# A fused attention and two-MLP kernel: SBUF tiles moved to 512-byte starts, A's four slices set 1280 bytes apart

## The chip, the cores and the metric

The kernel runs on one core of one Trainium2 chip. Each of the core's partitions of SBUF (there are 128) holds its share of every tile as a run of bytes; where in the partition a tile starts is decided when the program is built. The metric is device time in microseconds (us) of one execution, the median of several runs.

## What is computed

All tensors are fp32. A Nystrom attention (4 batches, 8 heads, 576 tokens, head size 64, 32 landmarks) is followed by two MLPs on 2304 tokens of width 512:

```
q_lm, k_lm = means over 32 segments of 18 tokens
A, Bm, C   = softmax(q k_lm'), softmax(q_lm k_lm'), softmax(q_lm k')
Z          = six Newton steps towards the inverse of Bm
x          = A @ Z @ C @ v
x          = rms_norm(x) * g ;  y = (silu(x @ w_gate) * (x @ w_val)) @ w_out      # d_ff 1536
h          = y @ w_in ;         out = (s * relu(h)**2 + b) @ w_out2               # d_ff 2048
```

## The kernel before

One function builds the whole program. Every step is recorded as an operation with the engines it may run on, an estimated duration and a key; a list scheduler (class `Scheduler`, `run`) then issues the operations in an order that is fixed at build time. Each engine walks its own list and waits on semaphores.

The large products use three fp32r matmuls for one fp32 product. `split` (lines 1115 to 1121) cuts an operand into a high part (L1117 on ScalarE or L1118 on VectorE) and a low part (L1119), and the matmuls add high times high, high times low and low times high (`PART3`, line 1244). Each of them loads its own 128x128 block of weights, the stationary operand, and then streams 256, 288 or 512 columns, the moving operand, past it. The matmul lines in question are:

- L1326 in `first_mm` (line 1319), the first MLP's gate and value products. Moving: a slice of A, 288 columns, from a tile of `xh` (high) or `xl` (low). Stationary: u (weights with the attention folded in), from `u_all` or from the free columns of `xh` and `xl`. 4 batches x 12 blocks of d_ff x 2 halves x 2 parts x 6 = 1152 matmuls.
- L1390 in `out_mm`, the first MLP's output product. Moving: `hh` or `hl` (the hidden block). Stationary: `w_all`. 528 matmuls of 512 columns and 144 of 256.
- L1282 in `product`, the second MLP's input product, which takes seven products instead of eight per pair of token blocks. Moving and stationary from `region`, `u_all`, `xh` and `xl`. 2 x 8 x 7 x 6 = 672 matmuls of 512 columns.
- L1417 in `second_mm`, the second MLP's output product. Moving: the output weights, from `w_all`, `region` or `u_all`. Stationary: `hh` or `hl`. 16 x 18 x 3 = 864 matmuls of 512 columns.
- L1664 in `plain`, the last token block's input product, 192 matmuls of 256 columns; moving from `region`, stationary from `xh` or `xl`.

Together that is 3552 fp32r matmuls: 2064 of 512 columns, 1152 of 288 and 336 of 256. The other matmuls (the attention's, the folding of the weights at L1299, the first blocks of the output product at L1372) are plain fp32.

A is stored in `attention` (lines 1092 to 1103). Its four slices, one for each pair of head group `g` and half `hf` of a segment, lie side by side in one tile of `xh` and one of `xl`, 288 columns (`HC`, 1152 bytes) each:

```
cols = slice(2 * HC * g + HC * hf, 2 * HC * g + HC * hf + HC)
```

SBUF is laid out in the order in which tiles are asked for, in the pool `sb` first and `region` in the pool `rp` behind it. Each tile starts at the next multiple of 32 bytes. The small tiles at the head of `sb` (masks, scalars) leave everything behind them 352 bytes past a multiple of 512, and `hmore` (3456 bytes) and `hbuf` shift what follows once more.

Of the kernel before, what the change touches and what calls it, by code (L numbers as in the profile page):

```python
# [7 lines left out]
F32 = mybir.dt.float32  # L8
F32R = mybir.dt.float32r
# [97 lines left out]
class Scheduler:  # L107
# [10 lines left out]
    def op(self, alts, key, fn, r=(), w=(), pair=False):  # L118
        if isinstance(alts, tuple):
            alts = {alts[0]: alts[1]}  # L120
        names = list(r) + list(w)
        bufs = {id(b): b for b in (x[0] if isinstance(x, tuple) else x for x in names) if isinstance(b, Buf)}
        o = Op(alts, key, fn, list(bufs.values()), pair)
        for b in o.bufs:
            b.left += 1
        deps = {}
        for x in r:
            if x in self.writer:
                deps[id(self.writer[x])] = self.writer[x]
        for x in w:  # L130
            if x in self.writer:
                deps[id(self.writer[x])] = self.writer[x]
            for y in self.readers.get(x, ()):
                deps[id(y)] = y
        for x in w:
            self.writer[x], self.readers[x] = o, []
        for x in r:
            self.readers.setdefault(x, []).append(o)
        deps.pop(id(o), None)
        for d in deps.values():  # L140
            d.users.append(o)
            o.n_deps += 1
        self.ops.append(o)
        return o
# [122 lines left out]
def t_dve(n):  # L267
    return 0.065 + 0.00104 * n


def t_dve2(n):
    return 0.07 + 0.00052 * n
# [6 lines left out]
def t_act(n):  # L279
    return 0.055 + 0.00085 * n  # L280
# [15 lines left out]
def tile_nystrom_attention_two_mlps(  # L296
# [16 lines left out]
    B, H, S, D = q.shape  # L313
    NT, DM = out.shape
    M = 32
    SEG = S // M
    HB = SEG // 2
    HC = HB * M
    NP = HC // 3
    KD = DM // 128  # L320
    F1 = w_gate.shape[1] // 128
# [10 lines left out]
    sb = ctx.enter_context(tc.tile_pool(name="sb", bufs=1))  # L332
# [3 lines left out]
    def ring(n, shape, name, dtype=F32):  # L336
        return Ring([Slot(sb.tile(shape, dtype, name=f"{name}{i}")) for i in range(n)], True)
# [11 lines left out]
    gT = sb.tile([128, KD], F32, name="gT")  # L349
    s_sb = sb.tile([128, 1], F32, name="s_sb")  # L350
    b_sb = sb.tile([128, 1], F32, name="b_sb")
    xbuf = sb.tile([128, KD, NT], F32, name="xbuf")

    x_r = [ring(2, [128, KD, 512], nm, F32R) for nm in ("xh", "xl")]
# [11 lines left out]
    u1_r = [Ring(u.slots + m, True) for u, m in zip(u_r, u_more)]  # L366
    u3_r = [Ring(u.slots + m[1:], True) for u, m in zip(u_r, u_more)]
    gw_r = ring(2, [128, 128], "gw")
    hmore = sb.tile([128, 864], F32, name="hmore")
    N_H = 8  # L370
    hbuf = sb.tile([128, 1536 + N_H * 288], F32, name="hbuf")
    t1_r = Ring([Slot(hbuf[:, 288 * i:288 * i + 288]) for i in range(2)], True)
    hs_r = [ring(2, [128, 512], nm, F32R) for nm in ("hh", "hl")]

    R_COLS, T_COLS = 11776, 3392
    rp = ctx.enter_context(tc.tile_pool(name="rp", bufs=1))
    region = rp.tile([128, R_COLS], F32, name="region", tag="region")
    tail = sb.tile([128, T_COLS], F32, name="tail")
    r_at = [0]

    def rring(n, cols, queued=True):
        o = []
        for _ in range(n):
            x, c = (region, r_at[0]) if r_at[0] < R_COLS else (tail, r_at[0] - R_COLS)
            assert c + cols <= x.shape[1], (r_at, cols)
            o.append(Slot(x[:, c:c + cols]))
            r_at[0] += cols
        return Ring(o, queued)
# [6 lines left out]
    bd_r = rring(4, 128)  # L395
    A_r = rring(2, HC)
    AT_r = rring(4, HC)
    wbd_r = rring(1, 256)
# [8 lines left out]
    tT0_r = Ring(tT_r.slots + [Slot(far[:, c, 0:SEG * D]) for c in range(2)], True)  # L407
    A0_r = Ring(A_r.slots + [Slot(far[:, 2, HC * i:HC * i + HC]) for i in range(2)] + [Slot(far[:, 3, 640:640 + HC])], True)
    h_late = [Slot(xbuf[:, c, NT - HC:NT]) for c in range(KD)]
    for x in h_late:  # L410
        x.held = True
    h_main = [Slot(hbuf[:, c:c + HC]) for c in [HC * i for i in range(2, 5)] + [1536 + HC * i for i in range(N_H)]]
    h_more = [Slot(hmore[:, HC * i:HC * i + HC]) for i in range(3)]
    hq_r = Ring(h_main + h_more + h_late, True)
    eC0_r = Ring(eC_r.slots + [Slot(far[:, 2, 576:1152])], True)
# [17 lines left out]
    for n, c in enumerate(COMBOS):  # L433
        for kd in range(2):
            i = 2 * (2 * n + kd)
# [70 lines left out]
    def attention(b, t0, t1):  # L506
# [8 lines left out]
        def at(alts, pos, fn, r=(), w=(), pair=False):  # L515
            mine.append(op(alts, 0.0, fn, r, w, pair or set(alts) == {"dve", "pool"}))
            mine[-1].spare = {"dve": SPA if b else SPA0}
            if not first and "sp" not in mine[-1].alts:
                mine[-1].after = RELB
            at_ops.append(mine[-1])  # L520
# [4 lines left out]
        def near(n):  # L525
            return {"dve": t_dve(n)} if first else dp(n)

        pair = xs[1, b] = (Buf(x_r[0]), Buf(x_r[1]))

        def part(i):  # L530
            return pair[i].t.rearrange("p k n -> p (k n)")[:, 0:SEG * D]

        def piece(g, h):

# [181 lines left out]
        for it in range(6):  # L716
            pU = Buf(ps_r)
            n = 32 if it in (2, 5) else 64
# [292 lines left out]
        for hf in range(2):  # L1011
# [22 lines left out]
            for c in range(0 if b >= XB else KD):  # L1034
                g, pr = divmod(c, 2)
# [23 lines left out]
            def s_mm(_, pS=pS, xq=xq, n_sum=n_sum):  # L1059
# [5 lines left out]
                for j in range(3):  # L1065
                    for c in range(n_sum):
                        nc.tensor.matmul(
                            out=pS.t[0:NP, j:j + 1], lhsT=xq.t[:, HC * c + NP * j:HC * c + NP * j + NP],
                            rhs=ones[:, 0:1], start=(c == 0), stop=(c == n_sum - 1))
# [4 lines left out]
            def s_rec(e, pS=pS, rs=rs):  # L1074
                e.tensor_scalar(out=rs.t[0:NP, 0:3], in0=pS.t[0:NP, 0:3], scalar1=1.0 / DM, scalar2=1e-6, op0=ALU.mult, op1=ALU.add)
                e.reciprocal(out=rs.t[0:NP, 0:3], in_=rs.t[0:NP, 0:3])

            at(("dve", 0.34), p0 + 0.06, s_rec, r=[pS], w=[rs])
            at(("act", 0.2 if first else 1.4), p0 + 0.07, lambda e, rs=rs: e.activation(
                out=rs.t[0:NP, 0:3], in_=rs.t[0:NP, 0:3], func=ACTF.Sqrt), r=[rs, "table"], w=[rs, ("root", b, hf)])  # L1080
            if first and hf:
                at(("act", 1.4), 0.0, lambda e: e.activation(out=spare, in_=spare, func=ACTF.Tanh),
                   r=[("root", 0, 0), ("root", 0, 1)], w=["spare"])
            at(near(HC), p0 + 0.07, lambda e, rs=rs, dg=dg: e.tensor_tensor(
                out=dg.t[0:NP].rearrange("p (j c) -> p j c", j=3),
                in0=ident[0:NP, 0:NP].unsqueeze(1).to_broadcast([NP, 3, NP]),
                in1=rs.t[0:NP, 0:3].rearrange("p (j o) -> p j o", o=1).to_broadcast([NP, 3, NP]),
# [3 lines left out]
                r=[dg, "const"], w=[pR])  # L1091
            for g in range(2):
                a = AT[hf, g]
                cols = slice(2 * HC * g + HC * hf, 2 * HC * g + HC * hf + HC)
                at(("dve", t_dve(HC)), p0 + 0.08, lambda e, a=a, pR=pR: e.tensor_tensor(
                    out=a.t[:, 0:HC], in0=a.t[:, 0:HC], in1=pR.t[:, 0:HC], op=ALU.mult), r=[a, pR], w=[a])
                wh, wl = ([(pair[i], ("a", hf, g))] for i in range(2))
                at({"act": t_act(HC), "dve": t_dve2(HC)}, p0 + 0.09, lambda e, a=a, cols=cols: (
                    e.activation(out=part(0)[:, cols], in_=a.t[:, 0:HC], func=ACTF.Copy) if e is nc.scalar
                    else e.tensor_copy(out=part(0)[:, cols], in_=a.t[:, 0:HC])), r=[a], w=wh, pair=True)  # L1100
                at(near(HC), p0 + 0.1, lambda e, a=a, cols=cols: e.tensor_tensor(
                    out=part(1)[:, cols], in0=a.t[:, 0:HC], in1=part(0)[:, cols].bitcast(F32),
                    op=ALU.subtract), r=[a, wh[0]], w=wl, pair=True)
                if first and g and hf:
                    at(("pool", 0.1), p0 + 0.11, lambda e, cols=cols: e.tensor_copy(
                        out=mark, in_=part(1)[:, cols][:, 0:1].bitcast(F32)), r=wl, w=["sums"])
# [212 lines left out]
    def first_mm(key, b, part, hf, u, ps):  # L1319
        x = xs[1, b]  # L1320

        def mm(_):
            for g in range(2):
                for i, (a, y) in enumerate(PART3):
                    c = 2 * HC * g + HC * hf
                    nc.tensor.matmul(  # L1326
                        out=ps.t[:, 0:HC], lhsT=u[a].t[:, 256 * g + 128 * part:256 * g + 128 * part + 128],
                        rhs=x[y].t.rearrange("p k n -> p (k n)")[:, c:c + HC],
                        start=(g == 0 and i == 0), stop=(g == 1 and i == 2))

        op(("pe", 6 * t_mm(HC)), key, mm, r=[(y, g) for y in u for g in range(2)]
           + [(y, ("a", hf, g)) for y in x for g in range(2)], w=[ps]).mode = "r"
        u_ops.append(S_.ops[-1])
# [124 lines left out]
    o_at, n = {}, 0  # L1458
    for i, (j, f) in enumerate(outs):
        lag = min(LAG0, max(LAG1, LAG0 - (i - F1) // 2))  # L1460
        n = max(n + (i >= len(units)), i + lag if i < len(units) else 0)
# [238 lines left out]
    for i, x in enumerate(todo):  # L1700
        if x[0] == "in":
            p, g = x[1:]
# [3 lines left out]
            n = 2 * (g > 0) if p == 0 else 4  # L1706
            steps = 7
        else:
            if x[1] == 0:
                x_last(t - X_LEAD)  # L1710
            g = x[1]
            n, steps = 2 if g < F_G - 1 else 2, 2
# [4 lines left out]
        keys, k = [], 0  # L1717
# [65 lines left out]
```

## Time and profile before

| | |
|---|---|
| median of 3 runs | 827.8 us (826.54 to 829.6) |
| the profiled execution | 828.2 us, of which the span of instructions is 826.5 us |
| TensorE (PE) busy | 812.0 us, 98% |
| weight loads (PEld) busy | 654.0 us, 79% |
| VectorE (DVE) busy | 644.1 us, 78% |
| ScalarE (ACT) busy | 463.2 us, 56% |
| GpSimd (POOL) busy | 122.4 us, 15% |
[...]

PE and PEld are the two halves of TensorE's work, matmuls and the loads of their weights. A matmul's duration runs from its start to the end of its results, so successive matmuls overlap and the busy time counts their union. The pace of a run of matmuls is therefore read from the distance between starts, not from one's duration.

### The profile page before, as it was taken

To read this page: it belongs to the slowest core of one execution; us is meant where nothing else is said; L and a number is where in the kernel's file an instruction comes from. 1 tells how busy PE (TensorE), PEld (TensorE's weight loads), DVE (VectorE), ACT (ScalarE), POOL (GpSimd) and SP (SyncE) were. 2 spreads that over 40 slices of the span, in tenths; PEclk is the share of its full clock that TensorE was granted. 3 is DMA by queue.
4 is the path that set the end of the run, shared out by engine and by line. 5 is a ranking of instruction groups with operands and counts; after the bars stand their busy time and mean duration, and the time that the engine had idled before them with its cause. 6 is when DMAs were issued, how large, how long until landed. Compare 5 with 4: busy or idle time off the path is not lost.

```text
span 826.5 us, 16515 instructions
## 1 busy us (share of the span) xinstructions
PE 812.0 (98%) x6158; PEld 654.0 (79%) x6158; DVE 644.1 (78%) x1452; ACT 463.2 (56%) x971; POOL 122.4 (15%) x176
## 2 busy tenths in 40 slices
PE   8999999999999999999999999999999999999997
PEld 5577777887787777888888888887888888888886
DVE  6888988777787777898998899698766767665564
ACT  5755665443535334565547766578555556565553
POOL 1370365127311132210100000000000000000000
PEclk9999999999999999999999999999999999999999
DMA  9999998352443323489888772232422432254234
GB/s 280 339 309 393 256 301 250 133 148 78 135 141 106 113 77 91 140 277 264 283 249 267 228 251 97 87 102 76 129 77 76 116 89 90 73 159 138 64 90 128
DMA packets 88817, 138.44 MB, mean 168 GB/s; under 512 B 28064, under 2 KB 50592, under 8 KB 88736
## 3 DMA queue, kind: packets, MB, share of 16 engines
q1 hardware_dynamic: 88544, 137.12, 54.4%
q8 instruction: 48, 0.79, 0.4%
q14 instruction: 33, 0.27, 0.1%
q10 hardware_dynamic: 192, 0.26, 0.1%
HBM read 114.81 MB, written 22.54 MB: 166 GB/s over the span
## 4 chain that ended last, share of the span: by engine, by line
PE 79%; DVE 8%; DMA 6%; ACT 2%; issue 1%; POOL 1%; SPq 0%; DVEq 0%; ACTq 0%; POOLq 0%
PE bank L1417 23%; PE bank L1282 16%; PE bank L1326 14%; PE bank L1390 13%; PE bank L1664 3%; PE bank L1299 2%; DMA stage<-in_moe_w_out_dram 2%; DMA xbuf<-in_moe_w_val_dram 2%; PE bank L1372 1%; DVE w_all L1119 1%; PE bank L760 1%; PE bank L681 1%; DVE hl L1119 1%; DMA rawo<-kepto 1%; POOL region L586 1%
## 5 line engine op out<-in xcount | busy, mean ns | idle before, releaser
L1417 PE MATMUL bank<-w_all,hh 128*128 128x512 f32 x472 | 148.0, 394 | 0.0
L1390 PE MATMUL bank<-hh,w_all 128*128 128x512 f32 (+1 forms) x448 | 144.7, 379 | 0.2 <-DVE w_all L1119 0.2
L1417 PEld LDWEIGHTS bank<-w_all,hh 128*128 128x128 f32 x472 | 88.2, 188 | 20.3
L1390 PEld LDWEIGHTS bank<-hh,w_all 128*128 128x128 f32 x448 | 81.5, 188 | 24.8 <-issue 10.4
L1417 PE MATMUL bank<-w_all,hl 128*128 128x512 f32 x236 | 93.1, 394 | 0.0
L1326 PE MATMUL bank<-xh,u_all 128*128 128x288 f32 x400 | 87.6, 299 | 0.3
L1390 PE MATMUL bank<-hl,w_all 128*128 128x512 f32 (+1 forms) x224 | 83.0, 371 | 0.0
L1119 DVE TENSOR_TENSOR w_all<-rawo,w_all 128x512 fp32r<-128x512 f32 x85 | 60.2, 708 | 15.9 <-ACT w_all L1117 13.4
L1326 PEld LDWEIGHTS bank<-xh,u_all 128*128 128x128 f32 x400 | 66.1, 188 | 3.8 <-issue 1.0
L1343 ACT ACTIVATE hbuf<-bank 128x288 f32<-128x288 f32 x96 | 39.2, 408 | 49.9 <-PE bank L1326 46.6
L1326 PE MATMUL bank<-xl,u_all 128*128 128x288 f32 x200 | 59.0, 295 | 0.0
L1326 PE MATMUL bank<-xh,xl 128*128 128x288 f32 x184 | 54.3, 295 | 0.0
L1326 PE MATMUL bank<-xl,xh 128*128 128x288 f32 x184 | 54.2, 295 | 0.0
L1417 PEld LDWEIGHTS bank<-w_all,hl 128*128 128x128 f32 x236 | 44.3, 188 | 10.5
L1117 ACT ACTIVATE w_all<-rawo 128x512 fp32r<-128x512 f32 x54 | 34.0, 629 | 31.3 <-PE bank L1390 14.5
L1345 DVE SCALAR_TENSOR_TENSOR hbuf<-hbuf,bank 128x288 f32<-128x288 f32 x96 | 42.4, 442 | 8.4 <-ACT hbuf L1343 7.7
L1390 PEld LDWEIGHTS bank<-hl,w_all 128*128 128x128 f32 x224 | 42.2, 188 | 5.4 <-DVE hl L1119 0.3
L1117 ACT ACTIVATE hh<-hbuf 128x288 fp32r<-128x288 f32 (+9 forms) x73 | 27.2, 393 | 27.4 <-PE bank L1390 18.5
L1326 PEld LDWEIGHTS bank<-xl,u_all 128*128 128x128 f32 x200 | 37.6, 188 | 0.9
L1119 DVE TENSOR_TENSOR hl<-hbuf,hh 128x512 fp32r<-128x512 f32 (+9 forms) x74 | 35.4, 488 | 1.6 <-ACT hh L1117 0.3
L1282 PE MATMUL bank<-region,xh 128*128 128x512 f32 x144 | 35.9, 395 | 0.7 <-ACT hbuf L1603 0.7
L1585 ACT ACTIVATE xbuf<-xbuf,b_sb,s_sb 128x512 f32<-128x512 f32 (+1 forms) x34 | 26.0, 764 | 18.9 <-DVE xbuf L1596 18.3
(326 smaller groups left out, 1855.4 us busy)
## 6 DMA issues: line engine op xcount, KB each, us to landing
rawg<-keptg SPq DMA_DIRECT2D x36, 512.0 KB, 5.1
stage<-in_moe_w_out_dram SPq DMA_DIRECT2D x28, 511.8 KB, 5.4
rawo<-kepto SPq DMA_DIRECT2D x48, 256.0 KB, 3.0
rawg<-kept SPq DMA_DIRECT2D x24, 512.0 KB, 3.5
rawo<-kept SPq DMA_DIRECT2D x36, 256.0 KB, 2.7
stage<-in_moe_w_in_dram SPq DMA_DIRECT2D x15, 512.0 KB, 5.5
keptg<-rawg SPq DMA_DIRECT2D x12, 512.0 KB, 7.1
kept<-tail SPq DMA_DIRECT2D x24, 256.0 KB, 4.8
```

The costliest lines, as they stand in the source:

```text
L586: at(on(9 * D), pos, lambda e, x=x, y=y: e.tensor_tensor(out=y(), in0=x()[:, 0:9], in1=x()[:, 9:18], op=ALU.add), r=[s3] + (["sums"] if b ...
L1117: e.activation(out=hi(), in_=src(), func=ACTF.Copy) if e is nc.scalar
L1119: b = op({"dve": t_dve(n), "pool": t_pool(n)}, key, lambda e: e.tensor_tensor(out=lo(), in0=src(), in1=hi().bitcast(F32), op=ALU.subtract) ...
L1282: nc.tensor.matmul(out=ps.t, lhsT=a[h][:, 128 * kd:128 * kd + 128], rhs=x[kd][y].t, start=(first and kd == 0 and i == 0), stop=(last and k ...
L1299: nc.tensor.matmul(out=pU[g].t[m, 256 * j:256 * j + 256], lhsT=gw[b].t[p, m], rhs=r.t[p, :, 128 * k:128 * k + 128], start=True, stop=True)
L1326: nc.tensor.matmul(out=ps.t[:, 0:HC], lhsT=u[a].t[:, 256 * g + 128 * part:256 * g + 128 * part + 128], rhs=x[y].t.rearrange("p k n -> p (k ...
L1343: op(("act", t_act(HC)), tg, lambda e: e.activation(out=th.t[:, 0:HC], in_=pg.t[:, 0:HC], func=ACTF.Tanh, scale=0.5), r=[pg], w=[th])
L1345: op(("dve", t_dve(HC)), tg, lambda e: e.scalar_tensor_tensor(out=th.t[:, 0:HC], in0=th.t[:, 0:HC], scalar=1.0, in1=pg.t[:, 0:HC], op0=ALU ...
L1390: nc.tensor.matmul(out=A[c].t[:, 0:n], lhsT=w[a].t[:, 128 * c:128 * c + 128], rhs=hs[y].t[:, 0:n], start=(f == 0 and i == 0), stop=(f == F ...
L1417: nc.tensor.matmul(out=A[c].t, lhsT=hs[a].t[:, s], rhs=w.t[:, 512 * y:512 * y + 512], start=(f == 0 and i == 0), stop=(f == F2 - 1 and i = ...
L1585: e.activation(out=h.t[:, c:c + n], in_=h.t[:, c:c + n], func=ACTF.Identity, scale=s_sb, bias=b_sb) if e is nc.scalar
L1664: nc.tensor.matmul(out=ps.t[:, 0:n], lhsT=tot.t[:, 1024 * a + c:1024 * a + c + 128], rhs=xs[3, kd // 2][y].t[:, n * (kd % 2):n * (kd % 2) ...
```

## The change

```diff
+    A_COL = 320
...
     b_sb = sb.tile([128, 1], F32, name="b_sb")
+    sb.tile([128, 40], F32, name="align")
     xbuf = sb.tile([128, KD, NT], F32, name="xbuf")
...
     gw_r = ring(2, [128, 128], "gw")
+    hs_r = [ring(2, [128, 512], nm, F32R) for nm in ("hh", "hl")]
+    N_H = 13
+    hbuf = sb.tile([128, N_H * 288], F32, name="hbuf")
+    t1_r = Ring([Slot(hbuf[:, 288 * i:288 * i + 288]) for i in range(2)], True)
     hmore = sb.tile([128, 864], F32, name="hmore")
-    N_H = 8
-    hbuf = sb.tile([128, 1536 + N_H * 288], F32, name="hbuf")
-    t1_r = Ring([Slot(hbuf[:, 288 * i:288 * i + 288]) for i in range(2)], True)
-    hs_r = [ring(2, [128, 512], nm, F32R) for nm in ("hh", "hl")]
...
-    tail = sb.tile([128, T_COLS], F32, name="tail")
+    tp = ctx.enter_context(tc.tile_pool(name="tp", bufs=1))
+    tail = tp.tile([128, T_COLS], F32, name="tail")
...
-    h_main = [Slot(hbuf[:, c:c + HC]) for c in [HC * i for i in range(2, 5)] + [1536 + HC * i for i in range(N_H)]]
+    h_main = [Slot(hbuf[:, c:c + HC]) for c in [HC * i for i in range(2, N_H)]]
...
-            return pair[i].t.rearrange("p k n -> p (k n)")[:, 0:SEG * D]
+            return pair[i].t.rearrange("p k n -> p (k n)")[:, 0:4 * A_COL]
...
-                cols = slice(2 * HC * g + HC * hf, 2 * HC * g + HC * hf + HC)
+                cols = slice(A_COL * (2 * g + hf), A_COL * (2 * g + hf) + HC)
...
-                    c = 2 * HC * g + HC * hf
+                    c = A_COL * (2 * g + hf)
```

An unused tile of 160 bytes is put ahead of `xbuf`, `hh` and `hl` are placed ahead of `hbuf`, `hbuf` loses a gap of 96 columns inside it, `hmore` comes last in `sb`, and `tail` goes into a pool of its own behind `region`. `hbuf` still has 13 slots of 288 columns. A's slices start 320 columns (1280 bytes) apart in place of 288. No instruction is added or removed; the five engines' lists, their waits and every operand's shape and type stay as they were, and only addresses in SBUF differ. Where tiles start in a partition, as built, in bytes past a multiple of 512:

```
tile                                             before               after
ident, ones                                      128                  128
xbuf, xh, xl, rawg, rawo, stage, u_all, w_all    352                  0
hh, hl                                           224                  0
hbuf, tail                                       224                  0
hmore                                            352                  128
region                                           480                  0
A's slices (g0 hf0, g0 hf1, g1 hf0, g1 hf1)      352, 480, 96, 224    0, 256, 0, 256
```

The 128-column blocks of weights are 512 bytes long and lie end to end, and the 512-column moving blocks are 2048 bytes long, so these start at the same remainder as their tiles. Below, the **phase** of a matmul is the distance in bytes between the start of its moving operand and the start of the weights loaded beside it, modulo 256. By the table it is 0 or 128 before (352 and 96 against 480 and 224), and 0 everywhere after.

## Rows read from the trace of the kernel before

**Rows 1.** The page: span, busy time, and 40 slices of the span.

```profile
span 826.5 us, 16515 instructions
...
PEclk9999999999999999999999999999999999999999
DMA  9999998352443323489888772232422432254234
```

**Rows 2.** Busy time by stretch: engines with instruction counts, clock, DMA share, GB/s.

```profile
0.00:140.00 140.00, 133.01 (x1484) 96.45 (x1485) 116.78 (x328) 84.14 (x192) 54.93 (x77) 1.00 0.99 304
140.00:300.00 160.00, 159.37 (x1800) 126.48 (x1799) 123.82 (x344) 71.60 (x201) 44.07 (x67) 1.00 0.40 121
...
565.00:765.00 200.00, 200.00 (x919) 164.54 (x918) 137.95 (x247) 115.58 (x199) 1.65 (x1) 1.00 0.36 104
```

**Rows 3.** The page: chain that ended last, shares of the span by line.

```profile
PE bank L1417 23%; PE bank L1282 16%; PE bank L1326 14%; PE bank L1390 13%; PE bank L1664 3%; PE bank L1299 2%; DMA stage<-in_moe_w_out_dram 2%; DMA xbuf<-in_moe_w_val_dram 2%; PE bank L1372 1%; DVE w_all L1119 1%; PE bank L760 1%; PE bank L681 1%; DVE hl L1119 1%; DMA rawo<-kepto 1%; POOL region L586 1%
```

**Rows 4.** Groups by line and operands (moving, stationary): busy us, mean ns of one.

```profile
L1417 PE MATMUL bank<-w_all,hh 128*128 128x512 f32 x472 | 148.0, 394 | 0.0
...
L1282 PE MATMUL bank<-region,xh 128*128 128x512 f32 x144 | 35.9, 395 | 0.7 <-ACT hbuf L1603 0.7
...
L1282 PE MATMUL bank<-region,u_all 128*128 128x512 f32 x96 | 24.8, 393 | 0.0
L1282 PE MATMUL bank<-region 128*128 128x512 f32 x96 | 24.4, 391 | 0.0
...
L1417 PE MATMUL bank<-region,hh 128*128 128x512 f32 x56 | 17.4, 391 | 0.0
L1417 PE MATMUL bank<-u_all,hh 128*128 128x512 f32 x48 | 15.0, 394 | 0.0
...
L1282 PE MATMUL bank<-xh,xh 128*128 128x512 f32 x32 | 11.2, 391 | 0.0
```

**Rows 5.** Timeline of PE, L1417 and L1664: start us, us, what.

```profile
765.61 0.63 PE L1417 MATMUL bank<-region,hh 128*128 128x512 f32 x2
...
768.36 1.61 PE L1664 MATMUL bank<-region,xl 128*128 128x256 f32 x12
769.81 0.63 PE L1417 MATMUL bank<-u_all,hh 128*128 128x512 f32 x2
...
772.60 1.60 PE L1664 MATMUL bank<-region,xl 128*128 128x256 f32 x12
774.04 0.63 PE L1417 MATMUL bank<-w_all,hh 128*128 128x512 f32 x2
```

**Rows 6.** Timeline of PE, L1282, from other stretches of the second MLP.

```profile
558.16 2.91 PE L1282 MATMUL bank<-region 128*128 128x512 f32 x12
560.91 1.56 PE L1282 MATMUL bank<-region,xh 128*128 128x512 f32 x6
563.20 3.05 PE L1282 MATMUL bank<-region,xh 128*128 128x512 f32 x12 [0.73 <-ACT hbuf L1603]
566.09 0.63 PE L1417 MATMUL bank<-w_all,hh 128*128 128x512 f32 x2
```

**Rows 7.** Timeline of PE, L1326: 12 matmuls of half 0, then 12 of half 1.

```profile
358.25 0.30 PE L1326 MATMUL bank<-xh 128*128 128x288 f32 x1
...
359.83 0.29 PE L1326 MATMUL bank<-xh 128*128 128x288 f32 x1
...
361.43 0.39 PE L1390 MATMUL bank<-hh,w_all 128*128 128x512 f32 x1
```

**Rows 8.** The chain in order of time, its four longest DMA pieces: start us, us.

```profile
35.42 5.71 DMA xbuf<-in_moe_w_val_dram
...
48.23 8.60 DMA xbuf<-in_moe_w_val_dram
...
103.03 6.88 DMA stage<-in_moe_w_out_dram
...
119.35 10.11 DMA stage<-in_moe_w_out_dram
```

## The prediction

> **What bounds the kernel now.** I read the page first. The span is 826.5 us and the clock is granted in full in every slice, so no time can come from the clock [rows 1]. The profiled execution took 828.2 us, 0.4 us above the median of the runs, 827.8; the sum below is made against 828.2 and carried over to the median by taking off those 0.4 us. Half a per cent, about 4.1 us, is what a measurement of this kernel can tell from no change.
>
> Then the stretches [rows 2]. The first 140 us are a start-up in which the DMA engines are busy for a share of 0.99. From 140 us on TensorE has 159.37 of 160 us, and later 200 of 200 us: the end is set there by how fast matmuls follow one another. The chain of waits says the same: L1417, L1282, L1326, L1390 and L1664, the five fp32r lines, hold 23 + 16 + 14 + 13 + 3 = 69% of it [rows 3], some 570 us. So a change that moves addresses alone is worth what it does to that pace, plus what it does to the loads in the first 140 us.
>
> Does the pace depend on addresses at all? The trace has a natural experiment, since tiles of two phases (front section on the change) are used on the same lines. Starts on the timeline give the pace. On L1417 twelve matmuls whose moving operand is in `region` take from 765.61 to 768.36, 2.75 us or 229.2 ns each; twelve from `u_all` take from 769.81 to 772.60, 2.79 us or 232.5 ns each [rows 5]. The weights are `hh` and `hl` in both; the first pair is in phase (480 and 224), the second is not (352 and 224). On L1282 twelve with both operands in `region` take 558.16 to 560.91, again 2.75 us and 229.2 ns; twelve with `region` streaming past weights in `xh`, out of phase, take 563.20 to 566.09, 2.89 us or 240.8 ns [rows 6]. On L1326 half 0 is in phase with u and half 1 is not: 358.25 to 359.83 is 1.58 us for twelve, 131.7 ns each, and 359.83 to 361.43 is 1.60 us, 133.3 ns each [rows 7]. The grouped rows show it over many more: a matmul of 512 columns lasts 391 ns on average with `region` on both sides, with `region` and `hh`, and with `xh` on both sides; it lasts 394 or 395 with `w_all` and `hh`, `u_all` and `hh`, `region` and `xh` [rows 4]. One row is weaker than the others: `region` with `u_all`, out of phase, has 393.
>
> [...]
>
> **The change, part by part.** No instruction, wait or DMA is added, removed or moved on any engine, so SP's and the other queues issue what they issued. What changes is three things.
>
> First, the phase. After the change every pair is in phase. How many are not now, from the code and the table of starts: on L1417 every matmul whose moving block is not in `region`; the rows have 56 of `region` with `hh`, and with `hl` there are half as many, so 864 - 84 = 780. On L1390 all 528 of 512 columns (224 against 352). On L1282 each of the seven products has 96 matmuls; three stream `region` past sums in `xh` and `xl` (288), two stream it past weights that lie every second time in `u_all` (96), one streams `xh` past weights that lie every second time in `region` (48): 432. That makes 1740 matmuls of 512 columns. At 232.5 - 229.2 = 3.3 ns each this is 5.7 us. On L1326 half of the 1152, 576, at 133.3 - 131.7 = 1.6 ns: 0.9 us. The 336 of 256 columns (L1390, L1664) are all out of phase; L1664 runs at 120 ns (772.60 to 774.04, 1.44 us for twelve [rows 5]) and no row shows 256 columns in phase. Between nothing and 3.3 ns each I take 1.5, near the 288-column step, which is the nearest in length: 0.5 us. Together 7.1 us of TensorE time.
>
> How much of that reaches the end? The five lines hold about 570 us of the chain, while their matmuls at these paces take 2064 x 0.232 + 1152 x 0.1325 + 336 x 0.12 = 672 us. The rest of them ran while something else set the end. 570 / 672 = 85%, so 7.1 becomes 6.0 us. If TensorE gets ahead of VectorE some of it turns into waits; VectorE has 137.95 of 200 us in the late stretch [rows 2], so a gain of one per cent there still finds its operands ready.
>
> Second, the common start. Before, all of these tiles start 96 bytes past a multiple of 128, and afterwards at a multiple of 256. The trace shows no fp32r matmul at any other remainder of 128, so the price has to be bounded. Below: nothing, since the two in-phase pairs that differ in their remainder of 256 (`region` at 224, `xh` at 96) both last 391 ns [rows 4]. [...] I take nothing, by the row of the two pairs. The other end is that collisions get worse when every stream starts at the same remainder; the worst out-of-phase stretch above, 240.8 ns, prices that.
>
> Third, loads and everything else. DMA destinations move by 32 to 352 bytes. No load to such an address is in the trace; its effect is bounded by nothing on one side and, on the other, by the chain's four longest DMA pieces, 5.71 + 8.60 + 6.88 + 10.11 = 31.3 us [rows 8]. I take nothing, because the later stretches do not wait for DMA and the share of 0.99 in the first 140 us says how busy the engines are, not that a packet's address matters. The wider spacing of A, the shorter `hbuf` and the tile of 160 bytes cost nothing: they are space only, and VectorE, ScalarE and GpSimd get the same shapes.
>
> The sum: 828.2 - 6.0 = 822.2 for an execution like the profiled one, 821.8 against the median.
>
> **Rivals.** (a) *The common start matters as well.* If starts at multiples of 256 spare each fp32r matmul one more step of the size seen, 3.3 ns, that is 3552 x 3.3 = 11.7 us, 10.0 of it at the end: 811.8. [...] Against it: the two equal rows of 391.
>
> (b) *Nothing happens.* The pace may hang on which tiles are used (most in-phase rows have `region`), or the gain may be taken up by waits. Then 827.8. Against it: `xh` with `xh` is in phase, does not touch `region`, and has the 391 ns of the others. [...]
>
> (c) *Slower.* Stream and weight load now start at the same remainder in every matmul and collide more, not less. At 240.8 ns in place of 232 on all 2064 that is 18.2 us, 15.4 at the end: 843. It decides if the 512-column pace after the change is above 232.5. Against it: all three in-phase stretches are the faster ones.
>
> (d) *Loads get faster too.* If the four DMA pieces shrink by a fifth, 6.3 us go on top of the 6.0: 815.5. For it: that stretch is full of DMA. Against it: nothing shows a packet's time to depend on its address.
>
> **How the numbers follow.** The forecast has 0.55, (a) 0.19, (b) 0.15, (c) 0.04, (d) 0.07. The forecast's own range is 819.5 to 824.2, from a share of 85% to all of the 7.1 with a little noise downwards, and from two thirds of it upwards. The range from 810 to 826 takes in (a) and (d) and half of the way to (b), and leaves out (c), the upper part of (b) and a common start worth more than one step. Faster by over half a per cent means below 823.7: most of the forecast (0.48) with (a) and (d), 0.74. Within half a per cent: the rest of the forecast and (b), 0.21. Slower: (c) and a little of (b), 0.05.
>
> **What would show it.** Right: twelve matmuls of L1417 take 2.75 us whatever tile their weights come from, half 1 of L1326 takes the 1.58 us of half 0, the grouped rows of 512 columns come together at 391 ns, and the first 140 us stay as they are. For (a) these drop further, below 2.72 us for twelve. For (b) they keep two levels, or VectorE's share of the chain grows. For (c) they rise above 2.79 us. For (d) the work of the start-up ends earlier. The prediction is wrong if the pace does not become one, or becomes one and the end does not follow.

## The result, and the profile after

The changed kernel takes 820.4 us (median of 5 runs, 819.2 to 820.95) against 827.8 us (median of 5, 826.54 to 829.6). The ratio is 0.9902, with a 95% interval from 0.9883 to 0.9921: faster by 7.4 us, and the whole interval is clear of the half per cent that can be told from no change. The forecast was 821.8 us.

The profiled execution took 819.2 us with a span of 817.5 us, 9.0 us less than the span of before. All line numbers are three higher: L1420 is the old L1417, L1285 the old L1282, L1393 the old L1390, L1329 the old L1326 and L1667 the old L1664. First the page of the kernel after: its span, the clock, and the chain that ended last by engine and by line.

```profile
span 817.5 us, 16515 instructions
...
PEclk9999999999999999999999999999999999999999
...
PE 77%; DVE 11%; DMA 5%; ACT 3%; issue 1%; SPq 0%; DVEq 0%; ACTq 0%
PE bank L1420 22%; PE bank L1329 15%; PE bank L1285 14%; PE bank L1393 12%; PE bank L1302 3%; PE bank L1667 3%; DMA rawo<-kepto 2%; PE bank L1375 2%; DVE w_all L1122 2%; PE bank L763 1%; DVE hl L1122 1%; PE bank L684 1%; DVE hbuf L1348 1%; 
```

The clock is granted in full as before [rows 1], and TensorE still bounds the kernel: the five lines hold 66% of the chain where they held 69% [rows 3]. VectorE's share of it is 11%; the part on the rivals comes back to that. Then the stretches of the kernel after, with the columns of [rows 2].

```profile
0.00:140.00 140.00, 133.43 (x1490) 97.43 (x1491) 117.81 (x330) 84.60 (x193) 56.92 (x79) 1.00 0.97 307
...
565.00:765.00 200.00, 200.00 (x947) 168.17 (x947) 138.80 (x249) 118.11 (x205) 0.00 (x0) 1.00 0.35 106
```

TensorE is as full as before, 200 of 200 us in the last stretch, but gets 947 matmuls through where it got 919. Of the 28 more, 22 are L1667's short ones, which now fall into the stretch because everything comes earlier; counted in columns it is 2.0% more. So the same matmuls stand closer together. Now the groups by line and operands that answer to [rows 4].

```profile
L1420 PE MATMUL bank<-w_all,hh 128*128 128x512 f32 x472 | 145.6, 389 | 0.0
L1393 PE MATMUL bank<-hh,w_all 128*128 128x512 f32 x352 | 124.9, 403 | 0.0
...
L1285 PE MATMUL bank<-region,xh 128*128 128x512 f32 x144 | 35.4, 391 | 1.3 <-ACT hbuf L1606 1.2
...
L1285 PE MATMUL bank<-region,u_all 128*128 128x512 f32 x96 | 24.4, 389 | 0.0
L1285 PE MATMUL bank<-region 128*128 128x512 f32 x96 | 24.3, 390 | 0.0
...
L1420 PE MATMUL bank<-region,hh 128*128 128x512 f32 x56 | 17.3, 391 | 0.0
...
L1285 PE MATMUL bank<-xh,xh 128*128 128x512 f32 x32 | 11.2, 389 | 0.0
```

On the old L1417 and L1282 all pairs but one now stand at 389 to 391 ns; the one is `xh` with `xl`, 32 matmuls, 391 before and 393 now. The pairs in these rows that were out of phase came down by 4 or 5 ns, and one that was in phase already, `xh` with `xh`, came down by 2. The output product of the first MLP, L1393, has 403 after 405 and is the exception; the part on the terms comes back to it.

The pace is best read from the chain in order of time: a piece is a run of matmuls of one line, and where TensorE never idles the next piece starts as the last one ends. Three pieces of before, and its last run of matmuls (start us, us, what):

```profile
660.91 2.80 PE bank L1417 x12
663.70 2.80 PE bank L1282 x12
...
681.84 2.79 PE bank L1417 x12
...
791.06 30.60 PE bank L1417 x132
```

The pieces that answer to them in the kernel after, with one from its last part:

```profile
654.75 2.72 PE bank L1420 x12
657.47 2.72 PE bank L1285 x12
...
675.15 2.72 PE bank L1420 x12
...
757.73 2.75 PE bank L1420 x12
...
782.81 29.96 PE bank L1420 x132
```

Twelve matmuls of 512 columns went from 2.80 to 2.72 us, 233.3 to 226.7 ns each. The pattern of pieces repeats after 20.93 us before (660.91 to 681.84) and after 20.40 us now (654.75 to 675.15). The last 132 matmuls took 30.60 us, 231.8 ns each, and now 29.96 us, 227.0 ns each. In the last part of the program, beside L1667, all of L1420's pieces of twelve take the 2.75 us that only `region` with `hh` had there before [rows 5].

The first and the last start on a line say in which half of the program the time went. The columns are engine, operation, operands and count, then shortest, median and longest duration in ns, first and last start in us, and form. Before:

```profile
L1417 PE MATMUL bank<-w_all,hh x472: 387/393/404, 460.8 to 819.6; 128*128 128x512 f32 x158
...
L1417 PE MATMUL bank<-region,hl x28: 388/389/396, 732.4 to 821.3; 128*128 128x512 f32 x28
```

After:

```profile
L1420 PE MATMUL bank<-w_all,hh x472: 389/389/398, 458.1 to 810.8; 128*128 128x512 f32 x158
...
L1420 PE MATMUL bank<-region,hl x28: 388/389/389, 724.6 to 812.4; 128*128 128x512 f32 x28
```

The second MLP's output product begins 2.7 us earlier, and from there to its last matmul the time is 360.5 us before (821.3 - 460.8) and 354.3 now (812.4 - 458.1): 6.2 of the 9.0 us of span. Of the other 2.7 us, 1.1 were there by the first MLP's first long run of L1326. The chain of before, that run and the longest run of the line:

```profile
137.26 3.18 PE bank L1326 x24
...
233.21 6.36 PE bank L1326 x48
```

The chain of the kernel after:

```profile
136.19 3.16 PE bank L1329 x24
...
231.71 6.32 PE bank L1329 x48
```

It starts 1.07 us earlier (137.26 to 136.19). That much is also found in two kernels below that gained nothing in all (e5 at 136.03, e6 at 135.92), so I take it for what one execution differs from the next in its start-up, not for an effect of the change. From there to the second MLP's first matmul it was 323.5 us and is 321.9, 1.6 us less: 48 matmuls of 288 columns take 6.32 us, 131.7 ns each, where they took 6.36, 132.5 ns each.

### The profile page after: what moved, and what is told of

Same layout as the page of the kernel before. It is cut to its first block, busy times and chain, and to the rows that moved or that the text cites. A ratio compares the mean times of both kernels' runs of the same rounds, so it can differ in the third digit from the quotient of the medians.

```text
span 817.5 us, 16515 instructions
## 1 busy us (share of the span) xinstructions
PE 802.9 (98%) x6158; PEld 652.5 (80%) x6158; DVE 644.1 (79%) x1452; ACT 462.3 (57%) x971; POOL 122.6 (15%) x176
## 4 chain that ended last, share of the span: by engine, by line
PE 77%; DVE 11%; DMA 5%; ACT 3%; issue 1%; SPq 0%; DVEq 0%; ACTq 0%
PE bank L1420 22%; PE bank L1329 15%; PE bank L1285 14%; PE bank L1393 12%; PE bank L1302 3%; PE bank L1667 3%; DMA rawo<-kepto 2%; PE bank L1375 2%; DVE w_all L1122 2%; PE bank L763 1%; DVE hl L1122 1%; PE bank L684 1%; DVE hbuf L1348 1%; DMA kept<-tail 1%; DMA rawo<-kept 1%
## 5 line engine op out<-in xcount | busy, mean ns | idle before, releaser
L1420 PE MATMUL bank<-w_all,hh 128*128 128x512 f32 x472 | 145.6, 389 | 0.0
L1393 PE MATMUL bank<-hh,w_all 128*128 128x512 f32 (+1 forms) x448 | 144.0, 378 | 0.1
L1420 PEld LDWEIGHTS bank<-w_all,hh 128*128 128x128 f32 x472 | 88.1, 188 | 18.0
L1393 PEld LDWEIGHTS bank<-hh,w_all 128*128 128x128 f32 x448 | 81.6, 188 | 24.3 <-issue 10.4
L1420 PE MATMUL bank<-w_all,hl 128*128 128x512 f32 x236 | 91.8, 389 | 0.0
L1329 PE MATMUL bank<-xh,u_all 128*128 128x288 f32 x400 | 87.1, 299 | 0.3 <-DVE hbuf L1348 0.2
L1393 PE MATMUL bank<-hl,w_all 128*128 128x512 f32 (+1 forms) x224 | 82.8, 370 | 0.0
L1329 PEld LDWEIGHTS bank<-xh,u_all 128*128 128x128 f32 x400 | 66.0, 188 | 3.8 <-issue 1.0
L1329 PE MATMUL bank<-xl,u_all 128*128 128x288 f32 x200 | 58.9, 295 | 0.0
L1329 PE MATMUL bank<-xl,xh 128*128 128x288 f32 x184 | 54.1, 294 | 0.0
L1329 PE MATMUL bank<-xh,xl 128*128 128x288 f32 x184 | 54.1, 294 | 0.0
L1420 PEld LDWEIGHTS bank<-w_all,hl 128*128 128x128 f32 x236 | 44.3, 188 | 9.2
L1393 PEld LDWEIGHTS bank<-hl,w_all 128*128 128x128 f32 x224 | 42.2, 189 | 5.3 <-DVE hl L1122 0.4
L1329 PEld LDWEIGHTS bank<-xl,u_all 128*128 128x128 f32 x200 | 37.6, 188 | 0.9
L1285 PE MATMUL bank<-region,xh 128*128 128x512 f32 x144 | 35.4, 391 | 1.3 <-ACT hbuf L1606 1.2
```

Of the source, the lines that this page charges most:

```text
L1285: nc.tensor.matmul(out=ps.t, lhsT=a[h][:, 128 * kd:128 * kd + 128], rhs=x[kd][y].t, start=(first and kd == 0 and i == 0), stop=(last and k ...
L1329: nc.tensor.matmul(out=ps.t[:, 0:HC], lhsT=u[a].t[:, 256 * g + 128 * part:256 * g + 128 * part + 128], rhs=x[y].t.rearrange("p k n -> p (k ...
L1393: nc.tensor.matmul(out=A[c].t[:, 0:n], lhsT=w[a].t[:, 128 * c:128 * c + 128], rhs=hs[y].t[:, 0:n], start=(f == 0 and i == 0), stop=(f == F ...
L1420: nc.tensor.matmul(out=A[c].t, lhsT=hs[a].t[:, s], rhs=w.t[:, 512 * y:512 * y + 512], start=(f == 0 and i == 0), stop=(f == F2 - 1 and i = ...
```

## Experiments

The theory after the result: only the phase matters, the distance between the two operands' starts modulo 256 bytes, and zero is the fast value. The rivals: the common start at multiples of 512 does part of it (rival (a) of the prediction), the loads gained (d), or A's wider spacing carries the gain. The first four kernels ran on one chip, where before had a median of 828.64 us; the last three on another, where it had 827.61. Each is compared with before on its own chip.

**e1: the common start taken away, the phase kept.** On the kernel after:

```diff
-    sb.tile([128, 40], F32, name="align")
+    sb.tile([128, 64], F32, name="align")
```

> The changed kernel with all tiles behind the head of the pool moved on by 96 bytes: every pair stays in phase (phase 0), but all tiles start 96 bytes past a multiple of 512, the remainder of 128 that they had before. If the phase alone makes the gain: about 820.4 us, L1420 at 227 ns a matmul as in the changed kernel. If the common start makes a part of it (the changed kernel runs at 227 where the in-phase stretches of before ran at 229): L1420 back at 229 and about 3.5 us more, 824. If the common start makes all of it: 827.

Measured: 820.38 us, ratio 0.9898 (0.9872 to 0.9924), the same as the change itself. The last run of matmuls in the chain of e1:

```profile
784.83 29.96 PE bank L1420 x132
```

Its largest group:

```profile
L1420 PE MATMUL bank<-w_all,hh 128*128 128x512 f32 x472 | 145.5, 389 | 0.0
```

The tiles that stood at multiples of 512, operands and load destinations alike, now start 96 bytes past one, and 29.96 us and 389 ns are those of the kernel after. Rival (a) falls, and with it a gain from where loads land: in e1 they land at the remainder modulo 256 that they had before.

**e2: the common start kept, the phase taken away.** On the kernel after; `hh`, `hl`, `hbuf`, `tail` and `region` move to 128, the rest stays at 0:

```diff
+    sb.tile([128, 32], F32, name="shift")
     hs_r = [ring(2, [128, 512], nm, F32R) for nm in ("hh", "hl")]
```

> The changed kernel with a gap of 128 bytes ahead of hh and hl, so that these, hbuf, tail and region start 128 bytes past a multiple of 512 and xh, xl, u_all and w_all at a multiple: all starts stay multiples of 128, but the phase is 128 again where it was before on L1420, L1393, L1285 and L1667; L1329 stays in phase. If the phase makes the gain: L1420 with w_all at 232 ns, L1420 with region at 227, and 7 to 8 us of the second MLP come back: about 827. If multiples of 128 are what matters: 820.4 and 227 everywhere.

Measured: 827.05 us, ratio 0.9979 (0.9967 to 0.9992). On the same chip this is 6.7 us behind e1, from 32 columns of nothing. The last run of matmuls of e2:

```profile
789.15 30.60 PE bank L1421 x132
```

And its groups:

```profile
L1421 PE MATMUL bank<-w_all,hh 128*128 128x512 f32 x472 | 148.0, 394 | 0.0
...
L1286 PE MATMUL bank<-region,xh 128*128 128x512 f32 x144 | 35.9, 395 | 0.7 <-ACT hbuf L1607 0.7
...
L1421 PE MATMUL bank<-region,hh 128*128 128x512 f32 x56 | 17.4, 391 | 0.0
```

30.60 us, 394, 395 and 391 ns are the numbers of before, pair by pair [rows 4]. One part of the expectation missed: L1421 with `region` did not stay at 227 ns but runs at 228.9 from start to start, as in the kernel before. So the phase of the 512-column matmuls is nearly all of it. What is left to before, 1.6 us with an interval from 0.7 to 2.7, has room for the first MLP's L1326, which is in phase in e2 as it is in the kernel after.

**e3: A's spacing alone.** On the kernel before, only `A_COL` with its three uses (the last four hunks of the change but for the tiles):

```diff
+    A_COL = 320
...
-                    c = 2 * HC * g + HC * hf
+                    c = A_COL * (2 * g + hf)
```

> The kernel before with A's slices 1280 bytes apart and nothing else: tiles stay at 352, 224 and 480, A's slices are at 352, 96, 352, 96, so L1326 is in phase in both halves and the other lines are as before. By the phase: half 1 of L1326 falls from 133.3 to 131.7 ns, 0.9 us of 576 matmuls, about 827.0. If the spacing itself, or the remainder of 512, matters more: below 826. If it does nothing: 827.8.

Measured: 828.68 us, ratio 0.9991 (0.9977 to 1.0005). The line's longest run in the chain of e3:

```profile
234.94 6.32 PE bank L1327 x48
```

The run has the 6.32 us of the kernel after, so the spacing does bring the second half of A's slices into phase; but 0.04 us in 48 matmuls is about 1 us in 1152, and the time can't show that. By itself this part of the change can't be told from nothing.

**e4: whose weights count, those in use or those being loaded?** On the kernel after, `hl` alone moves to 128:

```diff
-    hs_r = [ring(2, [128, 512], nm, F32R) for nm in ("hh", "hl")]
+    hs_r = [ring(2, [128, 512], "hh", F32R)]
...
+    hs_r.append(ring(2, [128, 512], "hl", F32R))
     hmore = sb.tile([128, 864], F32, name="hmore")
```

> The changed kernel with hl alone 128 bytes past a multiple of 512 (it lies behind hbuf, ahead of hmore); everything else at 0 as in the changed kernel. It tells which weights the phase counts against. On L1420 the order is hh with the high weights' block, hh with the low one, hl with the high one. If the next weights count, which are loaded while a matmul streams: the second of each three is slow (its neighbour is hl), the first and third are fast; rows of hl stay at 389 ns, those of hh rise to about 392. If its own weights count: hl rises to 394 and hh stays at 389. Either way a third of L1420 and of the 512-column matmuls of L1393, 464 in all, at 4 to 5 ns: about 822.3.

Measured: 823.67 us, ratio 0.9941 (0.9918 to 0.9964), some 60% of the gain (5.0 us, where e1 has 8.3 on the same chip). The groups of e4:

```profile
L1421 PE MATMUL bank<-w_all,hh 128*128 128x512 f32 x472 | 147.0, 393 | 0.0
...
L1421 PE MATMUL bank<-w_all,hl 128*128 128x512 f32 x236 | 93.7, 397 | 0.0
```

Neither theory is right alone. L1421 goes through weights in the order `hh`, `hh`, `hl`. Starts counted over the trace, from one matmul of the line to the one that follows it directly, give three paces: `hh` followed by `hh` 227.3 ns (288 pairs, untouched), `hh` followed by `hl` 232.4 ns (288), and the start behind an `hl` 234.1 ns (287, of which 59 are at the end of a run and are followed by another line). So the next start comes late both when a matmul's own weights and when the next ones are out of phase with what it streams. At these paces L1421 loses 288 x 5.1 + 288 x 6.8 ns = 3.4 us. L1394, where `hl` is the moving operand of a third, adds about 0.6 us (231.5 ns over all its starts, 230.4 in e1), and e4 is 3.3 us behind e1. The chain agrees: a run of twelve takes 2.77 us on L1421, between the 2.72 and 2.80 above, and 2.72 on L1286, which does not touch `hl`:

```profile
700.55 2.72 PE bank L1286 x12
703.27 2.77 PE bank L1421 x12
```

**e5 and e6: other phases.** On the kernel after, two unused tiles and A's spacing put `hh` and `hl` at 64, `region` and `tail` at 96 (e5), or at 32 and 192 (e6):

```diff
-    A_COL = 320
+    A_COL = 312
...
+    sb.tile([128, 16], F32, name="shift")
...
+    sb.tile([128, 8], F32, name="shift2")
```

In e6 the three numbers are 304, 8 and 40.

> The changed kernel with hh and hl at 64, tail and region at 96 past a multiple of 512, the rest at 0, and A's slices 1248 bytes apart. Phases: L1421 with w_all 192, with region 32; L1394 64; L1286 with region against xh and u_all 96, within region 0; L1330 0 and 192 in half 0, 224 and 160 in half 1. If the cost grows with the distance from phase 0 up to 128: L1421 with w_all about half way, 229.7 ns. If every phase but 0 costs the whole: 232. If only 128 does: 227, and the time stays at 820.

> The same with hh and hl at 32, tail and region at 192, A's slices 1216 bytes apart. Phases: L1421 with w_all 224, with region 160; L1394 32; L1286 with region against xh and u_all 192; L1330 0 and 128 in half 0, 192 and 64 in half 1. If the cost grows with the distance: L1421 with w_all at 228 to 229 ns. If every phase but 0 costs the whole: 232. If only 128 does: 227.

Measured: e5 827.84 us, ratio 1.0001 (0.9991 to 1.0012); e6 827.5 us, ratio 1.0003 (0.9986 to 1.0020). The whole gain is gone in both. The durations of e5 by line and operands:

```profile
L1422 PE MATMUL bank<-w_all,hh x472: 389/394/398, 459.0 to 819.2; 128*128 128x512 f32 x158
...
L1422 PE MATMUL bank<-region,hh x56: 390/394/397, 731.0 to 820.6; 128*128 128x512 f32 x56
```

The same of e6:

```profile
L1422 PE MATMUL bank<-w_all,hh x472: 392/395/502, 459.2 to 818.4; 128*128 128x512 f32 x158
...
L1422 PE MATMUL bank<-region,hh x56: 388/397/502, 730.3 to 819.8; 128*128 128x512 f32 x56
```

On L1422 the phases are 192 and 32 in e5, and 224 and 160 in e6, and medians are 394 to 397 ns in all four; phase 128 gave a mean of 394 in e2. From start to start the four have 232.7 to 234.3 ns, and phase 128 has 232.7. On this line there is no slope towards zero: a phase of 32 bytes costs what 128 costs. Two cases differ. The output product of the first MLP (L1395 in both) runs, from start to start, at 230.3 ns with `hh` and `w_all` at phase 64 in e5, against 230.4 in phase, 233.0 at 32 and 232.3 at 128. L1287 of e6 has 40 pairs at phase 64 too, 230.8 ns, beside 233.3 at phase 192. So not every phase but zero costs the whole; 64 costs less. On L1395 it costs nothing on average; only from the tenth start of a run on is it behind, with 229.0 ns where the matmuls in phase have 227.0. And matmuls of 256 columns are faster at one phase out of the three tried, 192. The timeline of e6:

```profile
774.98 1.54 PE L1669 MATMUL bank<-region,xh 128*128 128x256 f32 x12
776.36 0.63 PE L1422 MATMUL bank<-w_all,hh 128*128 128x512 f32 x2
```

The timeline of the kernel after:

```profile
764.49 1.60 PE L1667 MATMUL bank<-region,xl 128*128 128x256 f32 x12
765.92 0.63 PE L1420 MATMUL bank<-w_all,hh 128*128 128x512 f32 x2
```

Twelve take 1.38 us at phase 192 (774.98 to 776.36), 115 ns each, and 1.43 us in phase (764.49 to 765.92), 119 ns each. Over all 176 starts L1669 has 115.3 ns in e6 and 119.4 in phase; at phase 96 (e5) it has 120.0 and at 128 (before) 119.5, so out of phase is not faster as such.

**e7: the smallest edit that makes the phase zero.** On the kernel before, only the gap of 96 columns inside `hbuf` is taken out; `hh` and `hl` go to 352, where the other tiles of the program start, and `region` to 96:

```diff
-    N_H = 8
-    hbuf = sb.tile([128, 1536 + N_H * 288], F32, name="hbuf")
+    N_H = 13
+    hbuf = sb.tile([128, N_H * 288], F32, name="hbuf")
...
-    h_main = [Slot(hbuf[:, c:c + HC]) for c in [HC * i for i in range(2, 5)] + [1536 + HC * i for i in range(N_H)]]
+    h_main = [Slot(hbuf[:, c:c + HC]) for c in [HC * i for i in range(2, N_H)]]
```

> The kernel before with the gap of 96 columns taken out of hbuf and nothing else. This moves hh and hl from 224 to 352 and region from 480 to 96, so that every pair but half 1 of A is in phase, while no tile stands at a multiple of 512. If the phase alone makes the gain: L1417 at 227 ns and all of the gain but A's part of 1 us, 821.4. If starts at multiples of 512 or the spacing of A are needed: 824 to 828.

Measured: 820.53 us, ratio 0.9916 (0.9893 to 0.9938). The chain of e7:

```profile
231.70 6.35 PE bank L1326 x48
...
784.54 29.96 PE bank L1417 x132
```

The last run has the 29.96 us of the kernel after, the 288-column run still about that of before (6.35). No tile starts at a multiple of 512 and A's slices lie as they lay. This is the gain of the change within its interval, so one gap of 384 bytes in the wrong place had cost it.

## Why the prediction was right, and where its terms were off

**The mechanism** is the one forecast: the pace hangs on the phase (the last 132 matmuls of the old L1417 take 29.96 us in e1 and 30.60 in e2), and nothing else in the change does anything that can be measured: 32 columns of padding in SBUF move e1's or the change's 820.4 us to e2's 827.05, with the same instructions. What inside the chip makes the difference is not shown by any run. That only the weights loaded beside a matmul count fits one half of e4, the 232.4 ns, and not the other: in its trace, as in those of before and after, the load of the next weights begins 2 to 4 ns after a matmul's start, so beside an `hl` matmul weights of `hh` are loaded, in phase, and that interval is the longest, 234.1 ns.

**The step of the 512-column matmuls was mis-sized, and is the term that failed.** I took 232.5 - 229.2 = 3.3 ns for each of 1740 [rows 5], 5.7 us. The step is larger on two lines and smaller on the third. Starts counted over the two traces as in e4, of all 512-column matmuls that another follows directly, means in ns:

| line before (after) | before, phase 0 | before, phase 128 | all before | after | x count |
|---|---|---|---|---|---|
| L1417 (L1420) | 228.9 | 232.7 | 232.3 | 227.2 | 5.1 x 864 = 4.4 us |
| L1282 (L1285) | 229.4 | 232.5 | 231.4 | 227.4 | 4.0 x 672 = 2.7 us |
| L1390 (L1393) | none | 232.1 | 232.1 | 230.4 | 1.7 x 528 = 0.9 us |

(Only matmuls that follow one another without a wait are counted. The two columns by phase take those whose own and next weights have the same phase, the column behind them takes all.) The sum is 8.0 us in place of 5.7. My price was a difference within the kernel before, and there even the pairs in phase stood at 229; with nothing out of phase around them they stand at 227. Twelve of `region` with `region` took 2.75 us before (558.16 to 560.91 [rows 6]) and in phase all the same; the timeline after has

```profile
553.80 2.88 PE L1285 MATMUL bank<-region 128*128 128x512 f32 x12
556.52 1.52 PE L1285 MATMUL bank<-region,xh 128*128 128x512 f32 x6
```

and 2.72 us (553.80 to 556.52). The starts inside these two runs show why: after, all twelve are 226 or 227 ns apart; before, behind out-of-phase matmuls, the first five take 228 to 236 ns, 231.6 on average, and only the next six 226 or 227. In e5 and e6 the pairs of L1287 that are in phase with their own and the next weights take 231.0 and 228.7. A mixture does not show its own floor. The rows I took from L1417 were besides from the last part, where the change leaves 2.75 us for twelve beside L1667, and not from the 250 us ahead of it, where 2.72 is reached. L1390 in phase stays at 230 for the same reason: its runs are short, and in each the first starts have not settled. Its longest run without a wait, of 25 starts, in the timeline of the kernel after (the rows between are left out):

```profile
411.85 0.39 PE L1393 MATMUL bank<-hh,w_all 128*128 128x512 f32 x1
...
413.69 0.62 PE L1393 MATMUL bank<-hh,w_all 128*128 128x512 f32 x2
...
417.08 0.61 PE L1393 MATMUL bank<-hh,w_all 128*128 128x512 f32 x2
```

The first eight take 1.84 us, 230 ns each, and the fifteen behind them 3.39 us, 226 ns each. Over the trace the first six starts of a run have 231.2 ns on average (231.8 before) and those from the tenth on 227.0 (232.3 before). What makes the pace take several matmuls to settle is open.

**The other terms.** L1326: 0.9 us forecast, 132.6 to 131.7 ns in the count, 1152 x 0.9 = 1.0 us; right. The 256 columns: 0.5 us forecast, and nothing came (1.43 us for twelve after, 1.42 to 1.45 before); the estimate from 288 columns did not carry over, and e6 even has the sign turned. Together 9.0 us in place of 7.1.

**What reaches the end.** I let 85% through. From the first long run of L1326 on, the time went down by 1.6 + 6.2 = 7.8 us of the 9.0 that TensorE was spared, 87%; in the medians it is 7.4, 82%. So 7.1 x 85% was low by its first factor. That the shares come so near is partly luck: 85% was a share of the chain over the whole program, and the 87% rests on leaving out the 1.1 us of the start-up. Part of the rest turned into waits, as the text allowed for: `region` with `xh` has 1.3 us of idle time before it instead of 0.7 [rows 4], released by ScalarE.

**The rivals.** (a): twelve did drop under the 2.75 us of the forecast, but to 2.72 and not below it, so they stop at the mark that I had given; e1 shows that the common start has no part even in that. (b) needed two levels to stay, and there is one. Its other mark, a larger share of the chain for VectorE, did come, 11% where the page of before has

```profile
PE 79%; DVE 8%; DMA 6%; ACT 2%; issue 1%; POOL 1%; SPq 0%; DVEq 0%; ACTq 0%; POOLq 0%
```

But e1, with the same gain, has 8% and e7 has 10%, so the share does not tell whether the gain reaches the end; some of it went into waits, as above. (c) took its price from 240.8 ns in the out-of-phase twelve of 563.20 [rows 6]. That was no collision but the cost of starting after a wait: the kernel after has such a run too, all in phase, after a wait of 1.21 us:

```profile
559.25 3.02 PE L1285 MATMUL bank<-region,xh 128*128 128x512 f32 x12 [1.21 <-ACT hbuf L1606]
562.11 0.62 PE L1420 MATMUL bank<-w_all,hh 128*128 128x512 f32 x2
```

It takes 2.86 us (559.25 to 562.11), where it took 2.89 after its wait before; a run without a wait takes 2.72. The first two starts alone are 337 ns apart there, and 335 before. (d) falls with e1, where load destinations at 96 instead of 0 change nothing (ratio 0.9898 beside the change's 0.9902), and with e7, which has the gain with `xbuf`, `rawg`, `rawo` and `stage` left at 352 as before; and the DMA share of the first 140 us is 0.97 after 0.99.

**What stays open.** In the kernel after, the step from 256 columns (L1667) to 512 (L1420) is 119.4 to 227.2 ns, 107.8 ns or 0.42 ns a column. If all 512 columns went at that rate they would take 215.6 ns, an estimate from these two paces, and 11.6 of the 227.2 would be left. No experiment touched these. Putting only the operands of the 256-column matmuls at phase 192 was not tried: 336 x 4 ns is 1.3 us at most, and could not have been told from nothing.

## What to carry to other kernels

Where TensorE is full and every matmul loads new weights, tabulate where each moving and each stationary operand starts, modulo 256 bytes, and lay the tiles out so that the two agree for the longest matmuls; which remainder it is did not matter here (0 after, 96 and 352 past a multiple of 512 in e1 and e7: 820.4, 820.38 and 820.53 us), and one stray gap in one tile put most of the pairs out. A pace read off the good pairs of a mixed kernel may understate the gain, since the matmuls ahead of them slow them too, here for some five starts (231.6 ns on average, then 226 or 227). Before a long stretch of starts is put down to a collision, look for a wait in front of it; here one put 335 to 337 ns between the first two starts.

## What the runs showed of the hardware that I had not expected

- On one line the effect is a switch and no slope: 512-column fp32r matmuls of the second MLP's output product start 227.2 ns apart at phase 0 (after), and 232.7 to 234.3 at 32, 128, 160, 192 and 224 (e2, e5, e6). Phase 64 was tried on two other lines alone and is cheaper there: 230.3 ns against 230.4 in phase and 233.0 at 32 on the first MLP's output product.
- It reaches over to the neighbour: with weights in phase in use and weights out of phase coming next, the next start comes after 232.4 ns instead of 227.3 (e4).
- It depends on the length: 256 columns take 115 ns from start to start at phase 192 (e6), 119 in phase (after) and 119 to 120 at phases 96 and 128 (e5, before).
- The in-phase pace has to settle: behind a wait, shorter matmuls or out-of-phase ones it takes from three to ten starts or more to reach 227 ns (three to more than ten on L1393 after, five on L1420 behind L1667 after, five on L1282 before). Until then they stand 224 to 240 ns apart, and behind a wait the first two up to 341.
